# Attention before two expert layers: the low halves of two key tiles in one VectorE instruction, the cluster masks on ScalarE, two halvings of the maxima where there were three, and the maxima planned one step further ahead

## The chip, the cores and the metric

One core of one Trainium2 chip. Times are device microseconds of a whole execution. TensorE (PE) does the matmuls and loads their weights, VectorE (DVE), ScalarE (ACT) and GpSimd (POOL) the elementwise work, SyncE (SP) issues nearly all DMAs. Every engine works through its own instructions in the order in which the program gives them.

## The reference, cut to what matters

Three layers follow one another. The first is attention over 2 batches and 8 heads, 768 positions, head size 64, in which a query sees only the keys of its own cluster:

```python
q_assign = np.argmax(np.einsum('bhsd,hcd->bhsc', q_n, c_n), axis=-1)
k_assign = np.argmax(np.einsum('bhsd,hcd->bhsc', k_n, c_n), axis=-1)
mask = q_assign[:, :, :, None] == k_assign[:, :, None, :]
scores = np.where(mask, scale * np.matmul(q, k.transpose(0, 1, 3, 2)), -1e9)
attn = np.exp(scores - np.max(scores, axis=-1, keepdims=True))
attn = attn / (np.sum(attn, axis=-1, keepdims=True) + 1e-09)
out = np.matmul(attn, v)
```

Then come a layer of 8 experts, where each of the 1536 tokens goes to the best one (`relu(x @ w1) @ w2`, times its gate), and a dense layer of 2048 hidden features with `h * tanh(softplus(h))`. All inputs are float32. The kernel gets float32 accuracy out of float16 matmuls by splitting numbers into a high and a low half.

## The kernel before, in words

The program has three stages: attention, the experts, the dense layer. Where the sections below give a window from 30 to 230 us, that is attention without its first and last heads.

Attention runs over 32 units: 16 heads, each with two blocks of 384 queries. Per head, `split` makes high and low halves of k, q and v (lines 517 to 567), and `cluster` finds the cluster of each position: logits on PE (line 592), then five small DVE instructions (lines 596 to 621) that end in a one-hot tile `e3`, and two that write it, scaled, into columns 64 to 79 of the k and q tiles: `kmask` (line 624, one times 57344 minus 57344) and `qmask` (line 627). The tiles are then transposed by a DMA each that SP issues (`KXT` and `QXT`, line 632). With the mask columns a product of k and q falls far below zero where the clusters differ.

Per unit, `maxp` computes, for each of three tiles of 128 queries, all 768 masked scores (line 663). From the fourth unit on (units 3 to 31, 29 of them) ACT copies them to SBUF as float16 (`ev`, line 672), and when the three tiles are there DVE takes the maximum by halves: 768 to 384, 384 to 192 and 192 to 96 elements a query (`halve`, line 679, operands of 3x384, 3x192 and 3x96 elements), then a reduction over the 96 that are left (`last`, line 683). `maxfin` writes the negative maximum into column 80 of the q tile (line 706) and SP issues another transpose (`Q2`, line 710). `scores` then computes the scores again with the maximum taken off, key tiles along the partitions, two of the six key tiles at a time (lines 737 and 738), and ACT writes the exponentials as float32 (`P32`, 768 elements, line 745). For the first four key tiles `plo` takes from the float32 values their upper 16 bits read as bfloat16 (`PH`), which leaves a float16 low half (`PL`, line 762): one instruction of 384 elements for each key tile, on DVE or on POOL. `av` multiplies by v (line 792): two key tiles in float32, four as three products of halves. `avfin` (lines 815 to 831) divides by the sum and splits the result.

The order on all engines is made at build time by a planner (class `Plan`). Each operation is handed to it with an engine, an assumed duration in ns, what it reads and writes, and the planner puts it into the first gap of that engine after its inputs are ready and a buffer is free; `best` does so for several ways (on ACT or on DVE, say) and takes the one that ends first, after a bias in ns is added to every way but the first. DVE and POOL may not overlap in the plan for most operations. What is planned earlier takes its gap earlier; the order of planning is by a step count `z` (three to a unit), from which each kind of operation is shifted (lines 897 to 916): the maxima by `lm` steps ahead, their `maxfin` by `lm - 1`, the clusters by `lc` = 16 and the splits by `ls` = 22 ahead, `plo` by `lp` steps behind the scores, `av` by `la` = 6 behind. For the first units `at` shortens what is ahead. Idle PE gaps are filled with matmuls that nobody reads (`idle_work`, lines 462 and 466). On the chip nothing is planned: each engine keeps the order and waits for semaphores.

The buffers around the change: three pairs of PSUM banks shared by the score and maximum matmuls (tag `s`), two `ev` and two `eh` tiles, eight `P32`, three `PL`, five `Q2`.

After attention come the gate, the choice of experts, a scatter of the tokens through POOL's DMAs (line 1130), a transposing load by SP (line 1398) and the experts' matmuls.

Of the kernel before, what the change touches and what calls it, by code (L numbers as in the profile page):

```python
# [10 lines left out]
F16 = mybir.dt.float16  # L11
I32 = mybir.dt.int32
BF16 = mybir.dt.bfloat16
AF = mybir.ActivationFunctionType
ALU = mybir.AluOpType
AX = mybir.AxisListType
# [15 lines left out]
QB = 57344.0  # L32
KB = 57344.0
# [8 lines left out]
    lagy=2, lago=5, wbufs=6, wf=6, w2=3, wi=2, wbias=1000.0, cbias=1000.0,  # L42
    gbias=-1500.0, lbias=-1000.0, ldb=2, slack=8000, xsl=0, defer=18, lobias=-500, xbias=300,
    hbias=300, evac=tuple(range(3, 32)), wi0=4, wis=5, p32=8, gstep=3, pbias=-500, iedge=60.0, zx=10,
    zs=2, zn=13, rest=300, lsl=1000.0, dsl=400.0, idur=100, iw=232, la=6, lm=8,
    lc=16, ls=22, ll=30, pt=1, r0=0.45, r1=50.0, nb=5, pb=3,
    qb=5, lp=3, profile=(320, 272, 240, 224, 192, 176, 160, 144), va=(112,), vbias=1000.0, ybias=1000.0, vf=3, vw=4,
    sbias=1000.0, plsl=30000, nl=1, abias=-20000.0, ol=2, wa=4, wb=4, vn=2,
    vz=86, vs=3, hsbias=500.0, obias=1000.0, nwi=4, nw=2, avw=225, fli=44, rsl=6000.0, lag0=5, lags=(), lasti=6, idl=30000, ask=2, pli=12, ob=4, pr=1.0, pr0=1.0, nwo=3, wo0=40, wos=8, hsl=200.0,
)  # L50

# [197 lines left out]
def dve1(n):  # L249
    return 1.042 * n + 68  # L250


def dve2(n):
    return 0.521 * n + 70
# [10 lines left out]
def pe(n):  # L265
    return n / 2.4


class Builder:
# [102 lines left out]
    def attention(self, ctx, rctx, pctx, plan, mkeep, extra, then):  # L372

        tc, nc, P = self.tc, self.nc, self.cfg
        q, k, v, cent = self.q, self.k, self.v, self.cent
        B, H, S, D, C, NT, BLK = self.B, self.H, self.S, self.D, self.C, self.NT, self.NB
        E = self.E

        late = rctx.enter_context(tc.tile_pool(name="late", bufs=1, side="right"))
# [4 lines left out]
        nbuf = P["nb"]  # L384
        QX = [late.tile([128, NT, 128], F16, name=f"QX{i}") for i in range(nbuf)]
        KX = [late.tile([128, NT, 128], F16, name=f"KX{i}") for i in range(nbuf)]

        NW = P["nw"]
# [5 lines left out]
        st, bf = {}, {}  # L394
# [61 lines left out]
        def bank(name, buf, n):  # L456
            t = ps.tile([128, 512], F32, name=name, tag="a", bufs=2)
            st["bank", buf] = t
            return t[:, 0:n]
# [113 lines left out]
        def cluster(i, part):  # L573
            b, h = heads[i]
            n = 2 * NT * C
            if part == 0:
                bf["pl", i], bf["mx", i], bf["e", i] = Buf("a", 2), Buf("mx", 2), Buf("e", 2)
                bf["pl", i].open = True

                def bank1():  # L580
                    if ("pl", i) not in st:
                        st["pl", i] = bank("pl", bf["pl", i], 2 * NT * C).rearrange("p (a t c) -> p a t c", a=2, t=NT)
                    return st["bank", bf["pl", i]]

                def logits():
                    QKT, CT = st["QKT", i], st["CT"]
                    bank1()
                    pl = st["pl", i]
                    for a in range(2):
                        for t in range(NT):  # L590
                            for j in range(2):
                                nc.tensor.matmul(pl[:, a, t], lhsT=QKT[:, a, t], rhs=CT[:, j, h * C:(h + 1) * C], start=(j == 0), stop=(j == 1))

                def top():
                    st["mx", i] = late.tile([128, 2, NT, 1], F32, name="mx", bufs=2)
                    nc.vector.tensor_reduce(out=st["mx", i], in_=st["pl", i], axis=AX.X, op=ALU.max)

                def equal():
                    st["e", i] = late.tile([128, 2, NT, C], F16, name="e", bufs=2)
                    nc.vector.tensor_tensor(out=st["e", i], in0=st["pl", i], in1=st["mx", i].to_broadcast([128, 2, NT, C]), op=ALU.is_equal)  # L600
                end = plan.op("PE", 650, logits, use=(bf["QKT", i], bf["CT"]), new=bf["pl", i])
                rest_before(end - 650, bf["pl", i], bank1)
                plan.op("VEC", dve1(n), top, use=bf["pl", i], new=bf["mx", i])
                plan.op("VEC", dve1(n), equal, use=(bf["pl", i], bf["mx", i]), new=bf["e", i])
            else:
                KXb, QXb = bf["KX", i], bf["QX", i]
                bf["KXT", i], bf["QXT", i] = Buf("KXT", P["qb"]), Buf("QXT", 4)
                e2, m2, e3 = Buf("e2", 2), Buf("m2", 2), Buf("e3", 2)


                def weigh():
                    st["e2", i] = late.tile([128, 2, NT, C], F16, name="e2", bufs=2)
                    nc.vector.tensor_tensor(out=st["e2", i], in0=st["e", i], in1=wts, op=ALU.mult)

                def top():
                    st["m2", i] = late.tile([128, 2, NT, 1], F16, name="m2", bufs=2)
                    nc.vector.tensor_reduce(out=st["m2", i], in_=st["e2", i], axis=AX.X, op=ALU.max)

                def equal():
                    st["e3", i] = late.tile([128, 2, NT, C], F16, name="e3", bufs=2)  # L620
                    nc.vector.tensor_tensor(out=st["e3", i], in0=wts, in1=st["m2", i].to_broadcast([128, 2, NT, C]), op=ALU.is_equal)

                def kmask():
                    nc.vector.tensor_scalar(out=KX[i % nbuf][:, :, 64:80], in0=st["e3", i][:, 1], scalar1=KB, scalar2=-KB, op0=ALU.mult, op1=ALU.add)

                def qmask():
                    nc.vector.tensor_scalar(out=QX[i % nbuf][:, :, 64:80], in0=st["e3", i][:, 0], scalar1=QB, scalar2=None, op0=ALU.mult)

                def turn(nm, X, bufs):
                    def emit():  # L630
                        T = late.tile([128, NT, 128], F16, name=nm, tag=nm, bufs=bufs)
                        nc.sync.dma_start_transpose(out=T, in_=X[i % nbuf].rearrange("p t c -> p (t c)"))
                        st[nm, i] = T
                    return emit
                plan.op("DVE", 175, weigh, use=bf["e", i], new=e2)
                plan.op("VEC", dve1(n), top, use=e2, new=m2)
                plan.op("DVE", dve1(n), equal, use=m2, new=e3)
                plan.op("DVE", 100, kmask, use=(e3, bf["KX0", i % nbuf]), add=KXb)
                plan.op("DVE", 100, qmask, use=(e3, bf["QX0", i % nbuf]), add=QXb)
                for nm, X, Xb, bufs in (("KXT", KX, KXb, P["qb"]), ("QXT", QX, QXb, 4)):  # L640
                    if i < P["pt"]:
                        flip(NT, lambda t, X=X: X[i % nbuf][:, t], lambda j, w, nm=nm, bufs=bufs: tile_of((nm, i), [128, NT, 128], nm, bufs)[:, w * j:w * j + w], Xb, bf[nm, i])
                    else:
                        plan.dma("SP", 672, turn(nm, X, bufs), use=Xb, new=bf[nm, i], turn=True)

        def maxp(u, t):
            i, blk = divmod(u, BLK)
# [32 lines left out]
                return f  # L680

            def last():
                nc.vector.tensor_reduce(out=mkeep[:, u], in_=st["eh", u][:, :, 0:96], axis=AX.X, op=ALU.max)
            end = plan.op("PE", 2 * pe(384), mm, use=(bf["QXT", i], bf["KXT", i]), new=pm)
            rest_before(end - 2 * pe(384), pm, lambda: bank2()[:, 0])
            if not st["evac", u]:
# [5 lines left out]
            if t == 2:  # L692
                eh = Buf("eh", 2)
                plan.op("DVE", dve2(3 * 384), halve(384), use=bf["ev", u], new=eh)
                for n in (192, 96):
                    plan.op("DVE", dve2(3 * n), halve(n), use=eh, add=eh)
                plan.op("VEC", dve1(3 * 96), last, use=eh, new=bf["mk", u])

        def maxfin(u):
            i, blk = divmod(u, BLK)  # L700
# [49 lines left out]
            plan.op("ACT", 695, exp32, use=s, new=P32)  # L750

        def plo(u, pr):
            for j in range(2):
                kt = 2 * pr + j
                if kt >= NT - NW:
                    continue

                def emit(eng, kt=kt, j=j):
                    def f():
                        if ("PL", u) not in st:  # L760
                            st["PL", u] = late.tile([128, NT - NW, 384], F16, name="PL", tag="PL", bufs=P["pb"])
                        eng.tensor_tensor(out=st["PL", u][:, kt], in0=st["P32", u, pr][:, j], in1=st["PH", u, pr][:, j], op=ALU.subtract)  # L762
                    return f
                a, b = [("DVE", 470, emit(nc.vector))], [("POOL", 956, emit(nc.gpsimd))]
                plan.best(b, a, bias=P["pbias"], use=bf["P32", u, pr], new=bf["PL", u] if kt == 0 else None, add=bf["PL", u])

        def av(u, t):
            i, blk = divmod(u, BLK)
# [134 lines left out]
        for z in range(3 * NU):  # L903
            at(z, P["lm"], maxp, z // 3, z % 3)
# [1302 lines left out]
```

## Time and profile before

| | us |
|---|---|
| median of 3 runs | 699.46 |
| the 3 runs | 700.8, 695.21, 699.46 |
| the profiled execution | 694.05 |
| its span, first to last instruction | 692.3 |
| busy in the span: PE, DVE, ACT, POOL | 645.5, 554.8, 492.5, 67.2 |

The profiled execution is 1.75 us longer than its span. Rows with a duration tell how long an instruction was in its engine, from its start to the end of its last write; the next one of the same engine often starts before that. So the time that an instruction takes from its engine is read from the starts of neighbouring rows. A row of a timeline that ends in "x2" holds two instructions in a row. The busy time of PE holds the matmuls that fill gaps, too.

### The profile page before, as it was taken

The numbers are of one execution on the slowest core, as the hardware profiler recorded it, in microseconds if no ns is written. First come the engines' busy times: TensorE is split into PE (matmuls) and PEld (weight loads), VectorE is DVE, ScalarE is ACT, GpSimd is POOL, SyncE is SP. The second block draws the span as 40 slices with busy tenths as digits, with TensorE's granted clock in tenths as the row PEclk, the third lists the DMA queues.
The fourth block names the chain that finished last, engine by engine and source line by source line (L and its number), as shares of the span: only waits on it lengthen the run. The fifth ranks groups of instructions, "written<-read, shape, count | busy, mean of one in ns | idle before, by whom it ended". The sixth has DMA issues, their size and how long they took to land. (4 is left out here: it accounts for less than half of the span.)

```text
span 692.3 us, 15431 instructions
## 1 busy us (share of the span) xinstructions
PE 645.5 (93%) x6065; PEld 456.6 (66%) x6065; DVE 554.8 (80%) x1198; ACT 492.5 (71%) x717; POOL 67.2 (10%) x109
## 2 busy tenths in 40 slices
PE   7799999999998966999999999899999999999994
PEld 5576777777776864678999887454555555555541
DVE  6979979999998965788989996889888899545442
ACT  4479979978577723676667675889988878756760
POOL 3200000002200022012000000000260000001303
PEclk9989989999999998999999999999999999999998
DMA  6887999886566258999878992222333221000102
GB/s 176 159 149 191 240 252 226 154 154 190 125 148 106 67 196 254 318 326 295 259 246 257 246 313 95 92 91 62 91 61 94 62 92 32 0 1 16 76 1 95
DMA packets 148961, 103.96 MB, mean 150 GB/s; under 512 B 92304, under 2 KB 131216, under 8 KB 148880
## 3 DMA queue, kind: packets, MB, share of 16 engines
q1 hardware_dynamic: 146576, 96.21, 53.6%
q0 software_dynamic: 2304, 6.69, 2.6%
q8 instruction: 49, 0.80, 0.5%
q14 instruction: 32, 0.26, 0.1%
HBM read 64.02 MB, written 17.51 MB: 118 GB/s over the span
## 5 line engine op out<-in xcount | busy, mean ns | idle before, releaser
L1873 PEld LDWEIGHTS <-gt 128*128 128x128 f16 x576 | 56.3, 98 | 65.1
L745 ACT ACTIVATE P<-s 128x768 f32<-128x768 f32 x96 | 77.8, 812 | 28.6 <-PE s L738 22.5
L1873 PE MATMUL po<-xd,gt 128*128 128x512 f16 x432 | 97.0, 379 | 0.0
L1785 PE MATMUL fh<-x2h,winh 128*128 128x384 f16 x256 | 84.3, 329 | 4.9 <-DVE hs L1804 3.0
L1470 PE MATMUL ph<-xt,wh 128*128 128x320 f16 (+7 forms) x512 | 82.8, 259 | 3.3 <-DMA xt<-xs 3.3
L1785 PE MATMUL fh<-x2l,winh 128*128 128x384 f16 x256 | 84.2, 329 | 0.0
L1785 PE MATMUL fh<-x2h,winl 128*128 128x384 f16 x256 | 84.1, 329 | 0.0
L1515 PE MATMUL py<-ht,wh 128*128 128x320 f16 (+7 forms) x512 | 82.3, 256 | 0.1
L1785 PEld LDWEIGHTS <-winh 128*128 128x128 f16 x512 | 50.4, 98 | 41.9 <-issue 6.8
L672 ACT ACTIVATE ev<-pm 128x768 f16<-128x768 f32 x87 | 70.1, 809 | 7.5 <-PE pm L663 7.3
L737 PE MATMUL s<-Q,KXT 81*128 81x384 f16 x192 | 64.2, 335 | 7.8 <-DMA Q<-QX 5.4
L1470 PE MATMUL ph<-xt,wl 128*128 128x320 f16 (+7 forms) x256 | 64.4, 259 | 2.1 <-DVE wl L1435 2.1
L1515 PE MATMUL py<-ht,wl 128*128 128x320 f16 (+7 forms) x256 | 63.8, 256 | 1.4 <-DVE wl L1435 1.3
L738 PE MATMUL s<-QKT 128*128 128x384 f16 x192 | 64.1, 334 | 0.0
L762 DVE TENSOR_TENSOR PL<-P 128x384 f16<-128x384 f32 x119 | 61.8, 558 | 0.0
L792 PE MATMUL pa<-VW,P 128*128 128x65 f32 x384 | 59.6, 279 | 1.2 <-DVE LG L989 0.5
L792 PEld LDWEIGHTS pa<-VW,P 128*128 128x128 f32 x384 | 54.2, 198 | 8.0 <-issue 2.1
L1470 PEld LDWEIGHTS <-wh 128*128 128x128 f16 x512 | 48.0, 99 | 5.5 <-issue 0.4
L1515 PEld LDWEIGHTS <-wh 128*128 128x128 f16 x512 | 47.6, 98 | 4.9 <-issue 0.3
L792 PE MATMUL pa<-VX,P 128*128 128x65 f16 x768 | 49.6, 196 | 0.0
L663 PE MATMUL pm<-KXT,QXT 80*128 80x384 f16 x192 | 48.3, 335 | 0.8 <-ACT KXT L448 0.5
L792 PEld LDWEIGHTS <-P 128*128 128x128 bf16 x768 | 48.3, 106 | 0.0
(278 smaller groups left out, 1393.6 us busy)
## 6 DMA issues: line engine op xcount, KB each, us to landing
w1f<-in_moe_w_dram SPq DMA_DIRECT2D x36, 512.0 KB, 4.8
w2f<-in_moe_w_dram SPq DMA_DIRECT2D x36, 512.0 KB, 5.2
w2s<-in_moe_w_in_dram SPq DMA_DIRECT2D x16, 512.0 KB, 5.5
w2s<-in_moe_w_out_dram SPq DMA_DIRECT2D x16, 512.0 KB, 3.4
xs<-zero SPq DMA_DIRECT2D x13, 576.0 KB, 4.0
xsave<-xd SPq DMA_DIRECT2D x12, 256.0 KB, 4.3
kf<-in_k_dram SPq DMA_DIRECT2D x7, 384.0 KB, 4.4
qf<-in_q_dram SPq DMA_DIRECT2D x7, 384.0 KB, 4.8
```

What stands on the lines that cost most here:

```text
L663: nc.tensor.matmul(pm[:, j, 0:384], lhsT=QXT[0:80, g], rhs=KXT[0:80, 3 * j:3 * j + 3].rearrange("c t p -> c (t p)"), start=True, stop=True)
L672: nc.scalar.activation(out=st["ev", u][:, t].rearrange("p (a c) -> p a c", a=2), in_=st["pm", u, t][:, :, 0:384], func=AF.Copy, scale=1.0 ...
L737: nc.tensor.matmul(s[:, j, 0:384], lhsT=KXT[0:81, kt], rhs=Q2[0:81].rearrange("c t p -> c (t p)"), start=True, stop=False)
L738: nc.tensor.matmul(s[:, j, 0:384], lhsT=QKT[:, 1, kt], rhs=QKT[:, 0, 3 * blk:3 * blk + 3].rearrange("c t p -> c (t p)"), start=False, stop ...
L745: nc.scalar.activation(out=st["P32", u, pr], in_=st["s", u, pr][:, :, 0:384], func=AF.Exp, scale=sc)
L762: eng.tensor_tensor(out=st["PL", u][:, kt], in0=st["P32", u, pr][:, j], in1=st["PH", u, pr][:, j], op=ALU.subtract)
L792: nc.tensor.matmul(pa[:, t], lhsT=lhs, rhs=rhs, start=(n == 0), stop=(n == len(mm) - 1))
L1470: nc.tensor.matmul(st["p", i], lhsT=w[:, kk, fs], rhs=xt[:, 2 * kk + a], start=(kk == 0 and n == 0), stop=(kk == KD - 1 and n == 2))
L1515: nc.tensor.matmul(py, lhsT=w[:, f2, dsl], rhs=x, start=(f == 0 and j == 0), stop=(f == NF - 1 and j == 2))
L1785: nc.tensor.matmul(ph[b][:, 0:HB], lhsT=t2[w][:, f, k // 3], rhs=t2["x2"][x][:, k // 3, c0:c0 + HB], start=(k == 0), stop=(k == 3 * KD - 1))
L1873: nc.tensor.matmul(t2["o"][k], lhsT=gt[:, a, ts_], rhs=t2["wo"][f][:, w], start=(first and j == 0), stop=(last and j == 2))
```

## The change

Four things, and two numbers of the planner with them.

1. `plo` issues one DVE instruction for both key tiles of a pair (768 elements) in place of two of 384. It has no POOL way any more. The pairs are planned two steps behind the scores (`lp` 3 to 2).
2. `kmask` and `qmask` get an ACT way, planned at 190 ns; DVE's is taken only where it would end more than 1500 ns earlier.
3. The halving from 192 to 96 is left out; the reduction runs over 192 elements a query.
4. The maxima are planned nine steps ahead in place of eight (`lm`).

```diff
-    ... la=6, lm=8,
+    ... la=6, lm=9,
-    qb=5, lp=3, ...
+    qb=5, lp=2, ... mbias=1500.0, ...
...
+                def kmask_a():
+                    nc.scalar.activation(out=KX[i % nbuf][:, :, 64:80], in_=st["e3", i][:, 1], func=AF.Copy, scale=KB, bias=-KB)
+                def qmask_a():
+                    nc.scalar.activation(out=QX[i % nbuf][:, :, 64:80], in_=st["e3", i][:, 0], func=AF.Copy, scale=QB)
...
-                plan.op("DVE", 100, kmask, use=(e3, bf["KX0", i % nbuf]), add=KXb)
-                plan.op("DVE", 100, qmask, use=(e3, bf["QX0", i % nbuf]), add=QXb)
+                plan.best([("ACT", 190, kmask_a)], [("DVE", 100, kmask)], bias=P["mbias"], use=(e3, bf["KX0", i % nbuf]), add=KXb)
+                plan.best([("ACT", 190, qmask_a)], [("DVE", 100, qmask)], bias=P["mbias"], use=(e3, bf["QX0", i % nbuf]), add=QXb)
...
-                nc.vector.tensor_reduce(out=mkeep[:, u], in_=st["eh", u][:, :, 0:96], axis=AX.X, op=ALU.max)
+                nc.vector.tensor_reduce(out=mkeep[:, u], in_=st["eh", u][:, :, 0:192], axis=AX.X, op=ALU.max)
...
-                for n in (192, 96):
+                for n in (192,):
...
-                plan.op("VEC", dve1(3 * 96), last, use=eh, new=bf["mk", u])
+                plan.op("VEC", dve1(3 * 192), last, use=eh, new=bf["mk", u])
...
         def plo(u, pr):
-            for j in range(2):
-                kt = 2 * pr + j
-                if kt >= NT - NW:
-                    continue
-                ...
-                        eng.tensor_tensor(out=st["PL", u][:, kt], in0=st["P32", u, pr][:, j], in1=st["PH", u, pr][:, j], op=ALU.subtract)
-                a, b = [("DVE", 470, emit(nc.vector))], [("POOL", 956, emit(nc.gpsimd))]
-                plan.best(b, a, bias=P["pbias"], ...)
+            n = min(2, NT - NW - 2 * pr)
+            if n <= 0:
+                return
+            ...
+                nc.vector.tensor_tensor(out=st["PL", u][:, 2 * pr:2 * pr + n], in0=st["P32", u, pr][:, 0:n], in1=st["PH", u, pr][:, 0:n], op=ALU.subtract)
+            plan.op("DVE", dve1(384 * n), emit, use=bf["P32", u, pr], ...)
```

## Rows read from the trace of the kernel before

**Rows 1.** the page: busy tenths of the engines in 40 slices of the span

```profile
PE   7799999999998966999999999899999999999994
...
DVE  6979979999998965788989996889888899545442
```

**Rows 2.** windows: from:to, length, busy us of each engine (instructions), PE clock, DMA

```profile
30.00:230.00 200.00, 189.04 (x2417) 147.21 (x2418) 181.60 (x562) 160.97 (x266) 12.88 (x14) 0.96 0.78 172
100.00:140.00 40.00, 38.90 (x519) 30.38 (x519) 37.34 (x111) 37.31 (x66) 1.71 (x2) 1.00 0.89 191
300.00:320.00 20.00, 20.00 (x169) 16.23 (x167) 17.61 (x33) 14.82 (x24) 2.77 (x1) 1.00 1.07 331
```

**Rows 3.** waits from 20 to 250: who for whom, us in total, times, longest

```profile
ACT P L745 <- PE s L738: 22.5, 43, 2.0
ACT xd L828 <- DVE x L822: 7.5, 8, 3.3
...
DVE eh L679 <- ACT ev L672: 6.7, 10, 1.7
PE s L737 <- DMA Q<-QX: 5.4, 5, 1.4
```

**Rows 4.** groups by line and shape, to 330 us: busy us, mean ns of one

```profile
L762 DVE TENSOR_TENSOR PL<-P 128x384 f16<-128x384 f32 x119 | 61.8, 558 | 0.0
...
L1470 PE MATMUL ph<-xt,wh 128*128 128x320 f16 x64 | 15.4, 322 | 3.3 <-DMA xt<-xs 3.3
...
L683 DVE TENSOR_REDUCE mkeep<-eh 128x3 f32<-128x288 f16 x29 | 13.1, 453 | 0.7
...
L679 DVE TENSOR_TENSOR eh<-eh 128x288 f16<-128x288 f16 x29 | 8.9, 307 | 0.8
...
L762 POOL TENSOR_TENSOR PL<-P 128x384 f16<-128x384 f32 x9 | 7.9, 882 | 206.9 <-ACT P L745 206.9
...
L617 DVE TENSOR_REDUCE m<-e 128x12 f16<-128x192 f16 x16 | 5.6, 352 | 0.3
```

**Rows 5.** timeline of DVE (start, us, line): two low halves in a row

```profile
124.67 1.02 DVE L762 TENSOR_TENSOR PL<-P 128x384 f16<-128x384 f32 x2
125.61 0.35 DVE L831 TENSOR_TENSOR xd<-x,xd 128x192 f16<-128x192 f32 x1
```

**Rows 6.** timeline of DVE where POOL makes a low half at the same time

```profile
164.01 0.83 DVE L762 TENSOR_TENSOR PL<-P 128x384 f16<-128x384 f32 x1
...
182.44 1.65 DVE L762 TENSOR_TENSOR PL<-P 128x384 f16<-128x384 f32 x2
...
238.29 0.98 DVE L831 TENSOR_TENSOR xd<-x,xd 128x192 f16<-128x192 f32 x1
```

**Rows 7.** timeline of DVE: the two masks of a head and what follows

```profile
134.89 0.19 DVE L624 TENSOR_SCALAR KX<-e 128x96 f16<-128x96 f16 x1
134.99 0.18 DVE L627 TENSOR_SCALAR QX<-e 128x96 f16<-128x96 f16 x1
135.09 1.02 DVE L762 TENSOR_TENSOR PL<-P 128x384 f16<-128x384 f32 x2
```

**Rows 8.** timeline of DVE: the smaller halvings, the reduction and what follows

```profile
132.62 0.80 DVE L679 TENSOR_TENSOR eh<-eh 128x576 f16<-128x576 f16 x2
133.46 0.45 DVE L683 TENSOR_REDUCE mkeep<-eh 128x3 f32<-128x288 f16 x1
133.83 0.25 DVE L613 TENSOR_TENSOR e<-e,wts 128x192 f16<-128x192 f16 x1
```

**Rows 9.** timeline of ACT: a small copy and what follows it

```profile
71.69 0.29 ACT L564 ACTIVATE VW<-vf 128x128 f32<-128x128 f32 x1
71.89 0.51 ACT L517 ACTIVATE QK<-kf 128x384 f16<-128x384 f32 x1
```

**Rows 10.** waits of SP's queue to 250: us in total, times, longest

```profile
SPq L632 <- DVE KX L624: 6.7, 3, 3.5
```

**Rows 11.** windows, the gap-filling matmuls of line 462 alone: length, busy us

```profile
30.00:230.00 200.00, 9.71 (x61) 6.14 (x61) 0.96 0.78 172
```

More of the change, by code (lines that the diff above doesn't have):

```diff
@@ L44 @@
     hbias=300, evac=tuple(range(3, 32)), wi0=4, wis=5, p32=8, gstep=3, pbias=-500, iedge=60.0, zx=10,
-    zs=2, zn=13, rest=300, lsl=1000.0, dsl=400.0, idur=100, iw=232, la=6, lm=8,
+    zs=2, zn=13, rest=300, lsl=1000.0, dsl=400.0, idur=100, iw=232, la=6, lm=9,
     lc=16, ls=22, ll=30, pt=1, r0=0.45, r1=50.0, nb=5, pb=3,
-    qb=5, lp=3, profile=(320, 272, 240, 224, 192, 176, 160, 144), va=(112,), vbias=1000.0, ybias=1000.0, vf=3, vw=4,
-    sbias=1000.0, plsl=30000, nl=1, abias=-20000.0, ol=2, wa=4, wb=4, vn=2,
+    qb=5, lp=2, profile=(320, 272, 240, 224, 192, 176, 160, 144), va=(112,), vbias=1000.0, ybias=1000.0, vf=3, vw=4,
+    sbias=1000.0, plsl=30000, nl=1, abias=-20000.0, ol=2, mbias=1500.0, wa=4, wb=4, vn=2,
     vz=86, vs=3, hsbias=500.0, obias=1000.0, nwi=4, nw=2, avw=225, fli=44, rsl=6000.0, lag0=5, lags=(), lasti=6, idl=30000, ask=2, pli=12, ob=4, pr=1.0, pr0=1.0, nwo=3, wo0=40, wos=8, hsl=200.0,
@@ L752, in plo, with emit @@
         def plo(u, pr):
-            for j in range(2):
-                kt = 2 * pr + j
-                if kt >= NT - NW:
-                    continue
[L758 to L761, printed above, removed]
-                        eng.tensor_tensor(out=st["PL", u][:, kt], in0=st["P32", u, pr][:, j], in1=st["PH", u, pr][:, j], op=ALU.subtract)
-                    return f
-                a, b = [("DVE", 470, emit(nc.vector))], [("POOL", 956, emit(nc.gpsimd))]
-                plan.best(b, a, bias=P["pbias"], use=bf["P32", u, pr], new=bf["PL", u] if kt == 0 else None, add=bf["PL", u])
+            n = min(2, NT - NW - 2 * pr)
+            if n <= 0:
+                return
+            def emit():
+                if ("PL", u) not in st:
+                    st["PL", u] = late.tile([128, NT - NW, 384], F16, name="PL", tag="PL", bufs=P["pb"])
+                nc.vector.tensor_tensor(out=st["PL", u][:, 2 * pr:2 * pr + n], in0=st["P32", u, pr][:, 0:n], in1=st["PH", u, pr][:, 0:n], op=ALU.subtract)
+            plan.op("DVE", dve1(384 * n), emit, use=bf["P32", u, pr], new=bf["PL", u] if pr == 0 else None, add=bf["PL", u])
         def av(u, t):
```

## The prediction

> **What bounds the kernel now.** I began with the page. The reader is to see two kinds of stretches in its slices [rows 1]: in the second half PE is full and DVE at four to nine tenths, so nothing on DVE can matter there; in the first third, which is attention, both stand at eight or nine tenths. The chain that the page follows back from the end lies in the dense layer and is silent on attention. So I cut attention out with a window. From 30 to 230 us PE shows 189.0 of 200 us, DVE 181.6, ACT 161.0 [rows 2]. None is full. A stage like that is paced by the order in which three loaded engines hand work to each other, and an engine's saved time comes through only in part.
>
> Which of them is late? The list of waits, next, says that ACT's exponentials wait 22.5 us for score matmuls, DVE 6.7 us for ACT's copies, and PE only 5.4 us for the transposed maxima [rows 3]. PE's 189.0 also hold 9.7 us of gap-filling matmuls of one line alone [rows 11], and rows of matmuls overlap each other, so its figure is an upper end; DVE's is nearly real, since its rows follow each other closely. I take DVE as the engine that paces most of attention, with PE close behind. One stretch is different: from 100 to 140 us ACT has 37.3 of 40 us, as much as DVE [rows 2].
>
> What attention saves should reach the end: the first expert matmuls stand waiting 3.3 us for the tokens that attention's results are scattered into [rows 4], and from 300 us on PE is full with work of fixed size [rows 2].
>
> **Low halves.** Before, 119 run on DVE and 9 on POOL [rows 4]. Two in a row take 125.61 - 124.67 = 0.94 us until the next one starts, 0.47 each, though a lone one shows 1.02 - 0.47 = 0.55 [rows 5]. An element costs (453 - 352) / (288 - 192) = 1.05 ns on a reduction [rows 4]; I take the same here, so 384 elements are 0.40 us and the fixed part that the engine really pays is 0.07 us. A pair of 768 is then 0.94 - 0.07 = 0.87 us. Before: 119 x 0.47 = 55.9 us. After: 64 x 0.87 = 55.7. The merging alone gains 64 x 0.07 = 4.5 us and the nine halves that come back from POOL eat 9 x 0.47 = 4.2 of it. But POOL was no free help: where it made a half at the same time, DVE's own pair took 1.65 us for 1.02, a lone half 0.83 for 0.55, and a 0.35 us subtraction 0.98 [rows 5, 6], together 1.5 us that go too. Part: -1.7 us. Ends: if a pair costs twice a half, 64 x 0.94 = 60.2 against 57.4, +2.8; if it saves the whole fixed part of a lone row (0.55 - 0.40 = 0.15), 64 x 0.79 = 50.6, -6.8. I take the middle because two in a row are the nearest rows. The pair is ready as one, since one exponential writes both tiles.
>
> **Masks.** Two of them take 135.09 - 134.89 = 0.20 us of DVE [rows 7]; 16 heads x 0.20 = -3.2 us, with ends 0 (the planner keeps DVE's way wherever ACT would end over 1.5 us later) and 16 x 0.37 = -5.9 (their whole rows). On ACT the nearest row is a copy of 128 elements, 0.20 us to the next start [rows 9], so 32 x 0.20 = 6.4 us are added there. ACT's 39 idle us in the window cover that; from 100 to 140 us a fifth of it, 1.3 us, meets 2.7 idle ones, so there nothing can be gained. Two queues stand behind a mask: on ACT, exponentials that free the three PSUM pairs, and on SP the transposes of the masked tiles, which have held up its queue for 6.7 us in three waits before [rows 10]. Clusters are planned sixteen steps ahead, which covers this; without the cover see the second rival.
>
> **Halvings.** The halvings to 192 and 96 and the reduction take 133.83 - 132.62 = 1.21 us start to start [rows 8], because each waits for the result of the one before. The smaller halving is 0.31 us and the gap before it 0.03 [rows 4]; the reduction grows by 288 x 1.05 = 0.30. New chain: 1.21 - 0.34 + 0.30 = 1.17, so -0.04. In 23 of the 29 units the two halvings follow each other directly, as here, in one row; in six, other work lies between them. There the halving takes only 0.31 - 0.08 = 0.23 from the engine (0.08 is how far a row reaches past the next start, 133.46 + 0.45 - 133.83), and the unit loses 0.07. So 23 x -0.04 + 6 x 0.07 = -0.5 us; ends 29 x -0.04 = -1.2 and 29 x 0.07 = +2.0. The Trainium skill (VectorE: DVE Perf Modes, the perf-mode tier table) speaks against this edit: it gives float16 tensor_tensor twice the rate of a reduction, which has one rate only. By rate alone, 288 elements move from half to whole price, 0.15 us a unit or +4.4 us as an estimate from that page. The row of the reduction agrees on its rate, about one element a cycle, but the rate is not all that the chain pays.
>
> **Maxima a step ahead, low halves a step nearer.** The step moves two matmuls per tile, an ACT copy each, the DVE halvings, the write of the maximum and SP's transpose of Q2 past one step of loads and other transposes on SP's queue. It adds no work, so its price is a shift of waits: at best PE's 5.4 us for Q2 go [rows 3], at worst the ring of three PSUM pairs is held by maxima when scores are due. For the low halves, DVE does not wait for exponentials now; were it to wait as it does for the copies, +6.7 us [rows 3]. What is late next if Q2 is early is the exponential's score matmul, the 22.5 us. I cost both at nothing, with -5.4 and +6.7 as ends.
>
> **Sum.** DVE: -1.7 - 3.2 - 0.5 = -5.4 us. Of this I let through the share of attention in which ACT is not full (160 of 200 us) times DVE's busy share (0.91): 5.4 x 0.8 x 0.91 = 3.9 us. The profiled execution took 694.05 us (692.3 span and 1.75 around it): 690. It stands 5.4 us below the median of the runs shown, 699.46, so on the median's footing the forecast is 695.5 us, -0.6%. About 1%, 7 us, is what a measurement can tell from no change here.
>
> **Rivals.** *PE paces attention and DVE's saving turns into idle time.* For it: PE's nines, and that PE is seen to wait for so little. Against: fillers and overlap in its rows. Time: 699.5. The Trainium skill (Perfetto Trace Analysis, Identifying the Most-Contended Engine) would have PE judged by weight loads, not by matmul rows; those show 147.2 of 200 us [rows 2], which leaves PE room, and lowers this rival's chance. I give it 0.18.
>
> *ACT becomes the bound, slower.* The place: a mask at the head of ACT's queue that waits for DVE's one-hot tile, exponentials behind it, PSUM pairs not freed, PE without a bank. ACT's waits for DVE's normalised x show the size, 7.5 us in 8 [rows 3]. It decides from where masks and their waits exceed ACT's idle time in the full stretch, 2.7 us in 40, so 13.5 over attention: 6.4 of work and eight such waits just reach it. If the 6.4 us fall on the path and DVE's saving does not, 699.5 + 6.4 = 706; with the eight waits, 713. Against it: sixteen steps of lead. 0.15.
>
> *More than the sum.* The maxima ahead also take PE's waits for Q2 away: 3.9 + 5.4 = 9.3, so 690. For it: these waits are spread over the whole of attention, and DVE's relief makes the maxima earlier too. Against: the matmuls behind them may then wait for exponentials. 0.20.
>
> *The masks stay on DVE,* as the planner finds ACT late: 5.4 - 3.2 = 2.2, of which 1.6 come through, 697.9. It is 0.10 of the forecast's 0.47.
>
> **How the numbers follow.** The forecast's own range is 692 to 699. Over 1% faster (under 692.5) are the case of more and the lower end of the forecast, 0.20 + 0.10 = 0.30. Over 1% slower (above 706.5) is most of the ACT rival, and a little for the low halves waiting: 0.12. The rest, 0.58, is within. The range 686 to 704 holds the forecast, no gain, and most of more; it leaves out the ACT rival's upper part and the case in which the ends of the low halves and of the masks are both reached.
>
> **What would show it.** Right: 64 low halves near 0.95 us, none on POOL; a reduction near 0.75; about 30 masks on ACT near 0.29 us; DVE's busy time in attention down by some 5 us; the token scatter about 4 us earlier. Wrong: the scatter no earlier though DVE's time fell (PE paces), new ACT waits for line 621's tile (ACT), low halves that wait for exponentials, or masks still on DVE. A changed time that comes from the experts or the dense layer would make all of this beside the point.

## The result, and the profile after

| | before | changed |
|---|---|---|
| median, us (19 runs each, side by side) | 698.43 | 692.06 |
| ratio | 1 | 0.9914, 95% interval 0.9888 to 0.9940 |
| profiled execution, us | 694.05 | 690.03 |
| its span, us | 692.3 | 687.9 |

The changed kernel is 0.86% faster, 6.0 us by the ratio; the forecast was 3.9 us. Executions over 1.5% above the fastest of their kernel are left out of the ratios. The two profiled executions lie below their medians, by 4.4 us before and 2.0 us after, so they show 4.0 us of the gain.

The page of the changed kernel, the slices that answer to [rows 1]:

```profile
PE   7889999989999976999999998899999999999994
...
DVE  6799988979999874788998986889988899545542
```

Then the windows that answer to [rows 2], with the same columns:

```profile
30.00:230.00 200.00, 187.46 (x2443) 144.50 (x2442) 182.07 (x471) 165.42 (x290) 11.95 (x11) 0.98 0.81 174
100.00:140.00 40.00, 37.88 (x477) 28.26 (x475) 36.77 (x92) 36.40 (x67) 0.00 (x0) 0.96 1.03 194
300.00:320.00 20.00, 19.98 (x171) 16.43 (x170) 17.41 (x30) 14.04 (x25) 2.83 (x1) 1.00 1.04 305
```

The reader is to see that DVE is as busy as before in the same 200 us, because in a window of fixed length later work fills what was saved. ACT has 4.5 us more. The granted clock of PE is 0.98 in this execution and 0.96 in the one before. Of the two levels, 1.2 and 2.4 GHz, the lower is 0.5 here, so a mean of 0.96 is some 16 of 200 us at the lower level and 0.98 some 8.

What was saved shows in windows that end where the scatter of the tokens begins, before and changed:

```profile
0.00:254.76 254.76, 235.67 (x3046) 185.24 (x3046) 224.06 (x693) 190.00 (x321) 21.92 (x76) 0.97 0.74 169
0.00:251.31 251.31, 229.22 (x3002) 178.41 (x3002) 218.44 (x581) 191.75 (x344) 18.84 (x72) 0.97 0.76 171
```

Up to there DVE is busy 5.6 us less; behind it, 330.8 us before and 330.9 in the changed kernel.

The waits from 20 to 250 us, which answer to [rows 3]; the rows of L630 and L592 are new:

```profile
ACT P L751 <- PE s L744: 19.9, 32, 4.4
...
ACT KX L630 <- DVE e L621: 8.8, 8, 5.0
...
ACT xd L831 <- DVE x L825: 7.4, 9, 3.3
PE pl L592 <- DMA QKT<-QK: 7.0, 5, 1.8
...
DVE eh L685 <- ACT ev L678: 3.5, 7, 0.9
...
PE s L743 <- DMA Q<-QX: 1.9, 2, 1.1
```

PE's waits for Q2 fell from 5.4 to 1.9 us and DVE's for the copies from 6.7 to 3.5. ACT now waits 8.8 us for the one-hot tile, which is the second rival's wait, and PE 7.0 us for the transposes that the cluster logits read (`QKT`). All of PE's waits in this list together are 11.7 us before and 13.8 after: they did not become fewer, they moved.

The scatter of the tokens, in POOL's timeline of the changed kernel:

```profile
251.31 0.99 POOL L1133 DMA_INDIRECT xs<-xd,SLOT  x1 [26.14 <-DVE trk L1243]
```

and in that of the kernel before:

```profile
254.76 1.00 POOL L1130 DMA_INDIRECT xs<-xd,SLOT  x1 [15.70 <-DVE trk L1240]
```

It begins 3.45 us earlier, of 4.4 us by which the spans differ. So most of the time came from what stands ahead of the scatter. What follows it takes 437.5 us before and 436.6 after, and 435.7 to 437.4 in the four other orders of these two kernels that are run below.

### The profile page after: what moved, and what is told of

The parts are those of the page before. It is cut to its first block, busy times and chain, and to the rows that moved or that the text cites. A ratio compares the mean times of both kernels' runs of the same rounds, so it can differ in the third digit from the quotient of the medians.

```text
span 687.9 us, 15238 instructions
## 1 busy us (share of the span) xinstructions
PE 639.0 (93%) x6021; PEld 450.3 (65%) x6021; DVE 549.3 (80%) x1086; ACT 493.2 (72%) x740; POOL 64.2 (9%) x105
## 5 line engine op out<-in xcount | busy, mean ns | idle before, releaser
L767 DVE TENSOR_TENSOR PL<-P 128x768 f16<-128x768 f32 x64 | 60.5, 950 | 0.0
L795 PE MATMUL pa<-VW,P 128*128 128x65 f32 x384 | 56.9, 270 | 1.5 <-DVE x L825 0.9
L795 PEld LDWEIGHTS pa<-VW,P 128*128 128x128 f32 x384 | 52.8, 191 | 7.3 <-issue 1.6
L795 PE MATMUL pa<-VX,P 128*128 128x65 f16 x768 | 48.2, 194 | 0.0
L1438 DVE SCALAR_TENSOR_TENSOR wl<-w2f,wh 128x1024 f16<-128x1024 f32 x34 | 41.4, 1219 | 7.7 <-ACT wh L1430 7.7
```

The lines of the kernel that those rows point to most:

```text
L767: nc.vector.tensor_tensor(out=st["PL", u][:, 2 * pr:2 * pr + n], in0=st["P32", u, pr][:, 0:n], in1=st["PH", u, pr][:, 0:n], op=ALU.subtract)
L795: nc.tensor.matmul(pa[:, t], lhsT=lhs, rhs=rhs, start=(n == 0), stop=(n == len(mm) - 1))
L1438: nc.vector.scalar_tensor_tensor(out=t["l"], in0=t["f"], scalar=SW, in1=t["h"], op0=ALU.mult, op1=ALU.subtract)
```

## The experiments

The first theory was the prediction's: DVE's work paces attention, and what is taken from it comes through. The second: the new order, above all the maxima a step ahead, takes waits away, and the work counts for little. Later a third was needed: any new order moves the time. All ratios are to the kernel before, run beside, with 95% intervals.

**1. The three work edits in the old order.** The plan was made with the old costs; only what is issued differs.

```diff
-nc.vector.tensor_scalar(out=KX[...][:, :, 64:80], in0=st["e3", i][:, 1], ...)
+nc.scalar.activation(out=KX[...][:, :, 64:80], in_=st["e3", i][:, 1], func=AF.Copy, scale=KB, bias=-KB)
...
-plan.op("DVE", dve2(3 * n), halve(n), use=eh, add=eh)
+plan.op("DVE", dve2(3 * n), halve(n) if n > 96 else lambda: None, use=eh, add=eh)
...
-eng.tensor_tensor(out=st["PL", u][:, kt], ...)
+st["half", u, pr] = st.get(("half", u, pr), 0) + 1
+if st["half", u, pr] == 2:
+    nc.vector.tensor_tensor(out=st["PL", u][:, 2 * pr:2 * pr + 2], ...)
```

The `qmask` goes to ACT likewise, and the reduction runs over 192 elements.

> The kernel before, with three of the four edits written into its own order: the plan is made with the old costs, and only what is issued differs (masks on ACT at the place where DVE had them, the third halving left out, a pair's low half at the place of its second half, none on POOL). Theory 1, DVE's work paces attention and what is taken from it comes through: ratio to the kernel before about 0.992, as the whole change has. Theory 2, the new order (maxima a step ahead, everything planned again) takes away waits and the work counts for little: ratio 0.998 to 1.002.

Measured: 1.0154 (1.0113 to 1.0196), slower by 1.5%. Neither theory had this. Its windows show that DVE and ACT were busy for less of the 200 us, and PE at a clock of 0.92:

```profile
148.00:164.00 16.00, 15.95 (x166) 12.84 (x164) 8.22 (x21) 7.91 (x15) 0.00 (x0) 0.57 0.68 124
30.00:230.00 200.00, 181.80 (x2218) 139.82 (x2217) 166.74 (x433) 154.47 (x281) 6.62 (x6) 0.92 0.81 169
```

How one of these stretches begins is seen in the timelines of SP and of PE of this kernel:

```profile
140.54 1.54 SPq L632 DMA_TRANSPOSE KXT<-KX  x1
142.17 1.25 SPq L632 DMA_TRANSPOSE QXT<-QX  x1
143.51 1.68 SPq L710 DMA_TRANSPOSE Q<-QX  x1
```

```profile
147.45 0.34 PE L737 MATMUL s<-Q,KXT 81*128 81x384 f16 x1 [2.39 <-DMA Q<-QX]
147.62 0.33 PE L738 MATMUL s<-QKT 128*128 128x384 f16 x1
...
148.94 0.53 PE L738 MATMUL s<-QKT 128*128 128x384 f16 x1
```

DVE wrote the maximum of this Q2 at 137.35 us. SP went from one transpose to the next and issued it at 143.51; from issue to landing a Q2 takes 2.3 to 4.5 us in this run. PE stands 2.39 us for it; about 1.5 us later the same matmul takes 0.53 us where it took 0.33, and from 148 to 164 us the mean clock is 0.57. PE gets through 166 matmuls there, where the kernel before gets through 206 in the same 16 us. So this wait of PE was paid twice: once as the wait, once as the slow stretch behind it. Not every one is. PE waits 1.51 us for another Q2 in the same run, up to 228.85 us, and the clock behind it is full:

```profile
228.00:244.00 16.00, 14.40 (x204) 11.80 (x205) 12.01 (x27) 11.77 (x16) 0.00 (x0) 1.00 0.37 70
```

From 20 to 250 us PE waits 9.2 us for Q2, against 5.4 before.

**2. The step ahead alone.**

```diff
-la=6, lm=8,
+la=6, lm=9,
```

> The kernel before with nothing but the maxima planned nine steps ahead. Theory 1: 0.998 to 1.003, since no work goes. Theory 2: 0.992 to 0.994, PE's 5.4 us of waits for Q2 and ACT's 7.3 us for the maximum matmuls mostly gone.

Measured: 0.9986 (0.9954 to 1.0019), no gain that can be told. PE's waits for Q2 did fall; other waits of PE came, in its list of waits from 20 to 250 us:

```profile
PE pa L792 <- DVE x L822: 2.4, 3, 1.0
PE s L737 <- DMA Q<-QX: 2.2, 2, 1.3
PE pm L663 <- ACT P L745: 2.1, 4, 1.1
PE pl L592 <- DMA QKT<-QK: 2.0, 2, 1.8
```

**3. The changed kernel without the step.**

```diff
-la=6, lm=9,
+la=6, lm=8,
```

> The changed kernel with the maxima back at eight steps. Theory 1: still 0.991 to 0.994. Theory 2: 0.997 to 1.002.

Measured: 1.0014 (0.9980 to 1.0047). This speaks against the first theory: the 64 pairs, the shorter chain and the 32 masks on ACT are all there, DVE is busy 3.3 us less up to the scatter than in the kernel before, and no gain comes of it. Its waits from 20 to 250 us:

```profile
DVE eh L685 <- ACT ev L678: 7.7, 11, 2.5
PE s L743 <- DMA Q<-QX: 7.6, 6, 2.1
```

Run 2 speaks against the second theory in the same way. In these two orders the step and the edits pay only together.

**4. More work on DVE, nothing else.**

```diff
 nc.vector.tensor_reduce(out=mkeep[:, u], in_=st["eh", u][:, :, 0:96], axis=AX.X, op=ALU.max)
+nc.vector.tensor_reduce(out=mkeep[:, u], in_=st["eh", u][:, :, 0:96], axis=AX.X, op=ALU.max)
```

> The kernel before, order unchanged, with the last reduction of the maxima issued twice: 29 times about 0.4 us, 11.6 us more on DVE and nothing else. Theory 1: a share of 0.7 to 1 comes through, +8 to +12 us, ratio 1.011 to 1.017. If PE paces attention: under +4 us, ratio under 1.006.

Measured: 1.0086 (1.0050 to 1.0121). DVE's timeline shows what the second reduction takes, 0.49 us from start to start:

```profile
68.19 0.46 DVE L683 TENSOR_REDUCE mkeep<-eh 128x3 f32<-128x288 f16 x1
68.68 0.45 DVE L684 TENSOR_REDUCE mkeep<-eh 128x3 f32<-128x288 f16 x1
```

So 29 x 0.49 = 14.2 us were added, and 0.0086 x 700 = 6.0 us came through: a share of 0.42 (0.25 to 0.60 by the interval). That is neither DVE's full pace nor PE's. The work was added on the chain that the maxima wait for, and PE's waits for Q2 rose from 5.4 to 8.8 us; the same work elsewhere on DVE was not tried, so the later maxima and the fuller DVE are not told apart.

**5. As run 1, but the masks left on DVE.** The edit is that of run 1 without its first two lines.

> The kernel before with the merged low halves and the two halvings written into its own order, the masks left on DVE. The first run of this kind, with the masks on ACT as well, was 1.015. If the masks harm there (each puts 0.2 us and a wait in front of exponentials that were planned without it): 0.995 to 1.000 here. If the merged pair harms (its first half is ready only at the place of the second) or the half clock that follows PE's waits: 1.008 to 1.016, as before.

Measured: 1.0044 (1.0016 to 1.0073). This lies between the two cases. Masks on ACT in an order made for masks on DVE cost 1.0154 - 1.0044 = 1.1%. The merged pairs and the two halvings alone, in the old order, also gain nothing.

**6. The changed kernel with the masks on DVE.**

```diff
-plan.best([("ACT", 190, kmask_a)], [("DVE", 100, kmask)], bias=P["mbias"], ...
+plan.op("DVE", 100, kmask, ...
```

(and the same for the other mask)

> The changed kernel with the masks back on DVE, planned again, 3.2 us of DVE's work given back. By the sum of the prediction a share of 0.73 comes through, +2.3 us over the changed kernel: ratio to the kernel before 0.995. By the theory that the order drawn by the planner decides more than the work: anything from 0.988 to 1.004.

Measured: 0.9965 (0.9925 to 1.0004), near the 0.995 of the sum, but the other case allowed this too.

**7 and 8. A new order with the same edits.** One planned cost of each kernel is moved a little.

```diff
-plan.best([("ACT", 190, kmask_a)], ...
+plan.best([("ACT", 200, kmask_a)], ...
```

```diff
-plan.op("DVE", 100, kmask, ...
+plan.op("DVE", 105, kmask, ...
```

(and the same for the other mask in each)

> The changed kernel with the planned cost of a mask on ACT set from 190 to 200 ns: the same instructions but for a few that the planner moves between engines, in another order. If the gain belongs to the four edits: 0.989 to 0.994, like the changed kernel. If it belongs to the order that was drawn: off by 0.4% or more, 0.996 to 1.003.

> The kernel before with the planned cost of a mask on DVE set from 100 to 105 ns, nothing else. If an order drawn anew changes little: 0.998 to 1.002. If the order decides: off by 0.4% or more either way.

Measured: 0.9878 (0.9821 to 0.9935) for the changed kernel, 0.9952 (0.9922 to 0.9982) for the kernel before. The gain survives a new order; and the kernel before gains half a per cent from a change of 5 ns in a number that is only planned.

**9. The changed kernel with three halvings.**

```diff
-for n in (192,):
+for n in (192, 96):
...
-in_=st["eh", u][:, :, 0:192]
+in_=st["eh", u][:, :, 0:96]
```

> The changed kernel with the third halving and the short reduction back. By the sum of the prediction this edit was worth 0.5 us: 0.991 to 0.993, like the changed kernel. If a chain of three steps after the copies is what made the maxima late: 0.996 or more. By the rates alone (half price against full), the third halving would be better: 0.985 to 0.988. An order drawn anew moves about 0.5% either way, as the kernel before with a 5 ns change of one planned cost did.

Measured: 0.9894 (0.9863 to 0.9925), not told apart from the changed kernel.

**10. The changed kernel with the old low halves.** `plo` is that of the kernel before, on DVE or POOL, with `lp` = 3.

```diff
-nc.vector.tensor_tensor(out=st["PL", u][:, 2 * pr:2 * pr + n], ...)
+plan.best(b, a, bias=P["pbias"], use=bf["P32", u, pr], ...)
```

> The changed kernel with the low halves as before: one instruction a key tile, on DVE or POOL, planned three steps behind the scores. By the sum, 1.7 us given back, of which 1.2 come through: 0.993. If merging is what makes the changed kernel faster: 0.997 or more. If a pair as one block is a hindrance, as the run in the old order with masks on DVE suggested (1.004): under 0.990.

Measured: 0.9945 (0.9911 to 0.9979), 2.2 us worse than the changed kernel's ratio, between the first two cases.

**11 and 12. A third order of each.** A mask at 180 ns in the changed kernel, at 110 ns in the kernel before; the diffs are those of 7 and 8 with these numbers.

> The changed kernel with a mask planned at 180 ns, the other side of 190. A third order of the same edits. If the gain belongs to the edits: below 0.993. If the orders decide: anywhere between 0.987 and 1.000.

> The kernel before with a mask planned at 110 ns, a third order of the old edits. If the kernel before had merely drawn a bad order: 0.994 to 0.997 again. If the 105 ns order was a good draw: 0.999 to 1.003.

Measured: 0.9886 (0.9841 to 0.9932) and 0.9975 (0.9954 to 0.9996). The first is where the edits should put it; the second lies between its two cases.

Put together:

| | three orders | mean |
|---|---|---|
| old edits | 1, 0.9952, 0.9975 | 0.9976 |
| new edits, maxima a step ahead | 0.9914, 0.9878, 0.9886 | 0.9893 |

The means differ by 0.0083, 5.8 us of 699, while the orders of one kernel spread over 0.0048 and 0.0036. Every order of the new edits is faster than every order of the old. So the gain belongs to the edits with the step, and is about as large as the first comparison said. The third theory is right only as a noise of half a per cent. Versions 7, 9 and 11 are not shown to differ from the changed kernel.

The clock explains little of the gain. The mean granted clock over whole executions is 0.970 in the kernel before (84 executions, run beside the experiments) and 0.973 in the changed kernel (19), but 0.974 and 0.973 in runs 8 and 12, which have the old edits. Between executions of the kernel before, 0.01 of clock goes with 2.7 to 4.5 us, by a straight line through each of its three groups. So 0.003 would be about 1 us of the 6.0, an estimate.

## Why the prediction was right, and where its size was off

The forecast came out in direction and range, and its three pieces of work were priced well. How they reach the end was priced wrongly, so that the size came near is partly luck.

**Low halves.** As worked out. There are 64, none on POOL, and a pair takes 68.08 - 67.22 = 0.86 us to the next start, 0.87 foreseen. DVE's timeline of the changed kernel shows it, with the halving chain in front of it:

```profile
65.79 0.46 DVE L685 TENSOR_TENSOR eh<-eh 128x576 f16<-128x576 f16 x1
66.28 0.75 DVE L689 TENSOR_REDUCE mkeep<-eh 128x3 f32<-128x576 f16 x1
66.95 0.35 DVE L825 TENSOR_TENSOR x<-pa,dn 128x192 f32<-128x192 f32 x1
67.22 0.95 DVE L767 TENSOR_TENSOR PL<-P 128x768 f16<-128x768 f32 x1
68.08 0.55 DVE L526 SCALAR_TENSOR_TENSOR QK<-qf,QK 128x384 f16<-128x384 f32 x1
```

**Halvings.** The chain is 66.95 - 65.79 = 1.16 us, 1.17 foreseen, 1.21 before [rows 8]. By the rates alone the edit would have lost 4.4 us; run 9, which takes it back, is at 0.9894 against 0.9914, with overlapping intervals, so no such loss is seen. The Trainium skill (VectorE: DVE Perf Modes, the perf-mode tier table) gives a reduction one rate only, the lowest. The trace agrees on one rate: from 288 to 576 elements the row grows from 0.45 to 0.75 us, 1.04 ns an element, against 1.05 between two shorter ones. But here the shorter reduction needs one more dependent instruction in front of it, and that costs as much.

**Masks.** All 32 went to ACT:

```profile
L630 ACT ACTIVATE KX<-e 128x96 f16<-128x96 f16 x16 | 4.5, 281 | 12.0 <-DVE e L621 11.9
L633 ACT ACTIVATE QX<-e 128x96 f16<-128x96 f16 x16 | 4.3, 268 | 0.0
```

In ACT's timeline two of them take 70.12 - 69.76 = 0.36 us, 0.18 each and 5.8 in all, where 6.4 was foreseen:

```profile
69.76 0.28 ACT L630 ACTIVATE KX<-e 128x96 f16<-128x96 f16 x1 [0.51 <-DVE e L621]
69.95 0.27 ACT L633 ACTIVATE QX<-e 128x96 f16<-128x96 f16 x1
70.12 0.79 ACT L751 ACTIVATE P<-s 128x768 f32<-128x768 f32 x1
```

So the three terms of the sum, 5.4 us off DVE, were sized well, and DVE's busy time up to the scatter fell by 5.6. That figure also holds work that the planner moved: five subtractions (`xd`, line 834) now stand on POOL. So the 1.5 us by which POOL's work lengthened DVE's rows did not all go, as the low halves' term assumed: a halving beside one of the five takes 1.14 us where 0.75 is usual.

**The share let through was wrong, and so was the step at nothing.** The sum let 0.73 of DVE's saving through and "cost both at nothing" for the step ahead and the nearer low halves. Run 4 measured a share of 0.42 for work added, run 3 no gain for the work saved without the step, and run 2 none for the step without the work: two terms that do nothing alone gave 6.0 us together, where the forecast expected 3.9 from the first alone. What the step does to PE is seen in every order: from 20 to 250 us PE waits 1.7 to 3.0 us for Q2 in the seven versions with nine steps, and 3.4 to 9.2 in the seven with eight. The third rival, "more than the sum", named this wait, and put the sum at 9.3 us; the 6.0 measured lie between it and the forecast. But the fall of this wait is not where the 6.0 us went. All of PE's waits in these lists are 13.8, 12.4 and 12.7 us in the three orders of the new edits, and 11.7, 12.1 and 13.7 in those of the old: others took the place of those for Q2. How the step and the saving make up the gain together is not shown.

**PE paces attention:** not so in this simple form, as run 4 lost 6.0 us to instructions that were added on DVE. But PE's clock is a cost that the sum did not have: some 16 of 200 us at the lower level before, 8 after. At half rate, 8 us less would be some 4 us of PE's work. That is one profile of each, and the profile of run 7, a fast version, has 0.95; over all executions the clock is about 1 us of the gain, by the estimate above.

**ACT becomes the bound:** the wait came, 8.8 us from 20 to 250, and did not decide in the new order. In the old order masks on ACT do harm: run 1 against run 5 is a loss of 1.1%, 7.7 us, close to the 6.4 us of work that this rival priced. But its wait is not the reason there. In run 1 ACT waits for the one-hot tile only 0.2 us in all:

```profile
ACT KX L624 <- DVE e L621: 0.2, 1, 0.2
```

What differs are PE's waits for Q2, 9.2 us against 6.2 in run 5, and the mean clock of whole executions, 0.959 against 0.971. At some 4 us for 0.01 of clock, an estimate from the executions of these two versions, the clock would be more than half of the 7.7 us. Why masks on ACT make Q2 later is not shown.

**What stays open.** Each run that takes one edit back is one order. Against the mean 0.9893, taking back the step costs 1.2%, the masks 0.7%, the low halves 0.5%, the halvings nothing; these sum to far more than the gain of 0.8% between the means, so they are not shares of it, and half a per cent of each may be its order's. That neither the step nor the edits pay alone rests on runs 2 and 3, one order each.

## What to carry to other kernels

Where three loaded engines hand work to each other, price an edit's work and the lead that it can be turned into together: in the one order that was run of each, neither was worth anything alone. Do not put an instruction on another in-order engine without planning the order again; here masks moved within an old order cost 1.1%. And before a change of under 1% is put down to its edits, move a harmless planned number in both versions: it shows how far a new order alone carries.

## What the runs showed of the hardware

In run 1 a wait of PE of 2.39 us for Q2 was followed by 16 us at a mean granted clock of 0.57, in which matmuls of 384 columns took 0.53 us instead of 0.33. The kernel's filling matmuls did not cover that wait. It need not be a wait for Q2: in run 7, PE waited 1.59 us for `QKT`, and the next 16 us have the same 0.57:

```profile
140.97 0.76 PE L592 MATMUL pl<-CT,QKT 128*128 128x16 f16 x24 [1.59 <-DMA QKT<-QK]
...
142.07 0.44 PE L744 MATMUL s<-QKT 128*128 128x384 f16 x1
...
143.08 0.53 PE L743 MATMUL s<-Q,KXT 81*128 81x384 f16 x1
```

And a wait of 1.51 us in run 1 was followed by the full clock. So waits of about this length were followed by either.

The clock of one profile is no property of a version. The profiles of runs 1 and 4, the slowest versions, both have 0.92 in attention. But the profile of run 4 is one of its slowest executions (710.8 us, the median is 707.5), and the mean of the executions in its ratio is 0.972, no lower than the 0.969 of the kernel before beside it; for run 1 it is 0.959. The profile of run 12, which is faster than the kernel before, has 0.94.
